# A list scheduler gets a new cost table, a model of the transfer queue, and a table of 1128 shifted due times

## The chip, the cores and the metric

One NeuronCore of one Trainium2 chip runs the whole program in one launch. The metric is the time of one execution on the device in microseconds (us); lower is better. The core has a matrix engine (TensorE, PE in the rows), a vector engine (VectorE, DVE), a scalar engine (ScalarE, ACT), GpSimd (POOL) and a queue that issues transfers (SyncE, SP). Each engine works through its own list of instructions in the order in which the program holds them, and waits at an instruction whose inputs are not there yet.

## The reference, cut to what matters

```python
def _attn_ref(q, k, v, centroids):              # 2 x 8 heads, 768 rows, 64 columns
    q_assign = np.argmax(q_n @ c_n, axis=-1)    # nearest of 16 centroids, rows normalised
    k_assign = np.argmax(k_n @ c_n, axis=-1)
    mask = q_assign[:, :, :, None] == k_assign[:, :, None, :]
    scores = np.where(mask, scale * np.matmul(q, k.transpose(0, 1, 3, 2)), -1000000000.0)
    attn = np.exp(scores - np.max(scores, axis=-1, keepdims=True))
    attn = attn / (np.sum(attn, axis=-1, keepdims=True) + 1e-09)
    return np.matmul(attn, v)

def _moe_ref(x, w1, w2, w3, w_out):             # 1536 x 512
    return (x @ w1) * (x @ w2) @ w3 @ w_out

def _moe2_ref(x, w_in, w_out):
    h = x @ w_in                                # 1536 x 2048
    return (h * np.clip(h + 3.0, 0.0, 6.0) / 6.0) @ w_out
```

The weights of the two feed-forward parts arrive as 64-bit floats, and the kernel turns them into 32-bit ones on the chip.

## The kernel before, in words

The program first makes some thousands of small operations, each with a key, the engines that it may run on and a duration for each, the operations that it needs, the buffers (rings) that it takes and gives back, and a due time. Then `Plan.order` runs a list scheduler over them: it keeps a clock for each engine, picks among the operations that could start within 0.05 us of the earliest the one with the smallest due time, advances the clocks by the durations and by a table `LAT` of delays from engine to engine, and so writes down one order. The instructions of each engine are then emitted in that order. The durations and due times decide the order and, for operations that may run on several engines, the engine; the chip never sees them. A transfer counts in this plan as busy on the queue for its listed time, and its data as there a fixed `lat` later. A result counts as free for the next writer 0.3 us after its last reader.

The work goes through these stages, which overlap at their ends:

- Attention, 16 heads of six tiles of 128 rows. For each head: q and k are loaded, split into high and low parts (`qhi`, `qlo`, `khi`, `klo`), transposed (`Tq`, `Tk`, tiles ptqB and ptkB) and copied (`CqB`, `CkB`); passes with the centroids (`pa`) and a chain of eight small steps (`oh0` to `oh7`, tiles as and ohs) give a code for each row, which is transposed (`To`, tile pto) and copied (`Ck`, `Cq`) into the rows of the score operands. A score tile is written in two parts (`S1` and `S`, tile pst), its row maximum is taken on VectorE (`mx`, tile den), the exponential on ScalarE (`ex`, tile p), the result is transposed (`pT`, tile ptr), split (`ph` on ScalarE, `pl` on VectorE) and multiplied with v (`av`). There are two score banks: the second part of a tile waits for the exponential of the tile before.
- Beside it, w3 and w_out are converted from 64-bit (`c0` on ScalarE, `c1` on GpSimd or VectorE, `c3`, `c4`, `c5` on VectorE, tiles cvt and cvs), transposed and multiplied (tile psw), and later x @ w1 and x @ w2 of the first batch (tile psab) fill TensorE between the score tiles.
- From about 400 us on: the products psx (192 passes), then the second batch's psab, psx again, and a last stage of 16 rounds (`h`, tile psh, and `o`, tile po) that uses weights which are converted, stored to DRAM (tile set, transfer `sst`) and fetched again (tile m_gb, transfers `ff` and `wf`).

The last stage opens with the additions `ca` on VectorE (tile m_sn), which the fourth group of its passes waits for. The `Whl` splits and the reciprocals of the sums (`den_recip`, which the passes `prd` wait for) stand on VectorE at the end of the attention stage.

Of the kernel before, what the change touches and what calls it, by code (L numbers as in the profile page):

```python
# [26 lines left out]
LAT = {  # L27
    ("pe", "act"): 0.2, ("pe", "dve"): 0.2, ("pe", "pe"): 0.0, ("act", "dve"): 0.155, ("act", "pool"): 0.17,
    ("dve", "act"): 0.13, ("act", "pe"): 0.17, ("dve", "pe"): 0.24, ("pool", "pe"): 0.21, ("pool", "pool"): 0.1,
        ("dve", "dve"): 0.13, ("dve", "pool"): 0.155, ("pool", "act"): 0.08,  # L30
}

# [11 lines left out]
class Plan:  # L44
# [17 lines left out]
    def order(self):  # L62
        delta, bias = 0.05, {"dve": 0.3, "pool": -0.3}
        ops = self.ops
        left, users, src = {}, {}, {}
# [7 lines left out]
        slots = {r: [0.0] * c for r, c in self.rings.items()}  # L73
        free = dict.fromkeys(ENG, 0.0)
        port = {"dve": 0.0, "pool": 0.0}
        ready = {k: None for k, o in ops.items() if not left[k]}
        out = []
        while len(out) < len(ops):
            cand = {e: [] for e in ENG}
            for k in ready:  # L80
                o = ops[k]
                t = 0.0
                ok = True
                for r in set(o[6]):
                    c = o[6].count(r)
                    if len(slots[r]) < c:
                        ok = False
                        break
                    t = max(t, sorted(slots[r])[c - 1])
                if not ok:  # L90
                    continue
                best = None
                for e, d in o[1].items():
                    st = max(free[e], t)
                    for end, pe in src[k]:
                        st = max(st, end + LAT.get((pe, e), 0.08))
# [7 lines left out]
                cand[best[1]].append((best[2], o[5], o[9], k))  # L104
# [13 lines left out]
            for r in o[6]:  # L118
                slots[r].remove(min(slots[r]))
            end = st + o[1][e]  # L120
            free[e] = end
            if e == "pool" or e == "dve" and o[10]:
                port[e] = end
            for r in o[7]:
                slots[r].append(end + 0.3)
            out.append(k)
            for u, data in users.get(k, ()):
                if data:
                    src[u].append((end + o[8], e))
                left[u] -= 1  # L130
                if not left[u]:
                    ready[u] = None
        return [ops[k] for k in out]
# [3 lines left out]
def cluster_attention_moe_kernel(  # L137
# [174 lines left out]
    op(("idle", 0), "pe", 0.0, lambda: idle_pe(5), ("id",), due=-30)  # L312
    op(("idle", 1), "pe", 0.0, lambda: idle_pe(8), [("Tq", 1, 1), ("idle", 0)], due=-30)
    op(("idle", 2), "pe", 0.0, lambda: idle_pe(3), [("S1", 0, 2), ("idle", 1)], due=-30)
    op(("idle", 3), "pe", 0.0, lambda: idle_pe(5), [("Tq", 2, 1), ("S1", 0, 3), ("idle", 2)], due=-30)
# [108 lines left out]
    def prep_ops(h):  # L424
# [13 lines left out]
        for nm, d in (("q", -6.5), ("k", -5.7)):  # L438
            for hf in range(2):
                dd = b + d + 0.4 * hf  # L440
                op(("T" + nm, h, hf), "pe", 0.17, lambda nm=nm, hf=hf: stack_T(h, nm + "B", hf),
# [9 lines left out]
        for hf in range(2):  # L451
            dd = b - 1.8 + 0.5 * hf
            op(("To", h, hf), "pe", 0.17, lambda hf=hf: codes_T(h, hf), (("oh7", h), "id"), due=dd, take=("s",),
               drop=("oh",) if hf else ())
            fop("Co", ("Ck", h, hf), {"a": 0.375, "d": 0.47}, lambda e, hf=hf: codes_C(e, h, "k", hf),
# [3 lines left out]
        op(("pa", h), "pe", 1.3, lambda: assign_mm(h), [("CqB", h, 0), ("CqB", h, 1), ("CkB", h, 0), ("CkB", h, 1),  # L459
# [149 lines left out]
    def attn_ops(h):  # L609
        b = NC * h  # L610
        for c in range(NC):
# [6 lines left out]
            op(("S1", h, c), "pe", 0.43, lambda c=c: scores(h, c, 0), nd, due=t, take=("r",))  # L618
            op(("S", h, c), "pe", 0.22, lambda c=c: scores(h, c, 1), [("S1", h, c)] + prev, due=t + 0.1,
# [4 lines left out]
            op(("ex", h, c), "act", 0.88, lambda c=c: sexp(h, c), (("mx", h, c),), due=t + 0.6, take=("p",),  # L624
# [302 lines left out]
    def T(us):  # L927
        return GS + 2.0 + us / 4.1
# [626 lines left out]
```

## Time and profile before

| what | value |
|---|---|
| runs | median 786.06 us, 785.38 to 786.44 |
| profiled execution, first to last instruction | 785.5 us |
| TensorE busy | 762.6 us (97%), 4471 passes |
| VectorE busy | 659.7 us (84%) |
| ScalarE busy | 534.7 us (68%) |
| GpSimd busy | 258.2 us (33%) |
| granted TensorE clock, mean | 0.997 |

The profile gives the span of its execution and no other time of it; the median of the runs lies 0.56 us above that span. Passes on TensorE overlap, and the end of each is modelled: a pass of 384 columns is listed with some 0.34 us while the next one starts 0.17 us later. A gap between two starts that is shorter than the listed length does not show as idle time.

### The profile page before, as it was taken

What the parts mean: (1) busy time and instruction counts of PE and PEld (TensorE: products, weight loads), DVE (VectorE), ACT (ScalarE), POOL (GpSimd) and SP (SyncE); (2) the same over time, 40 slices, a digit from 0 to 9 for tenths busy, and PEclk for the clock granted to TensorE, in tenths of its full rate; (3) what the DMA queues carried; (4) which work ended last, traced back from release to release, by engine and by line L of the source; (5) the groups of instructions that cost most, each with busy time, mean ns of one, the idle gap of its engine ahead of it and who ended that gap; (6) DMA issues with size and microseconds to landing.
All of it is one profiled execution on the core that took longest, in us unless ns stands there. A gap on an engine that the chain in (4) does not pass through costs nothing.

```text
span 785.5 us, 12835 instructions
## 1 busy us (share of the span) xinstructions
PE 762.6 (97%) x4471; PEld 698.3 (89%) x4471; DVE 659.7 (84%) x1193; ACT 534.7 (68%) x1061; POOL 258.2 (33%) x277
## 2 busy tenths in 40 slices
PE   6799999999999999999999999999999999999997
PEld 5688887789899999999999999989898989888986
DVE  7998898999999897788998798979999976666742
ACT  5679897777877786767763565746776667555543
POOL 5733757344555454323232131611122111010100
PEclk9999999999999999999999999999999999999999
DMA  7443343333454441333344543366533424212102
GB/s 248 131 149 105 89 138 101 109 113 97 120 159 146 114 148 53 90 112 114 106 138 132 152 160 114 109 217 213 164 124 120 138 91 148 81 55 68 41 14 81
DMA packets 57041, 94.24 MB, mean 120 GB/s; under 512 B 5168, under 2 KB 33936, under 8 KB 56976
## 3 DMA queue, kind: packets, MB, share of 16 engines
q1 hardware_dynamic: 56976, 93.43, 38.4%
q8 instruction: 35, 0.57, 0.3%
q14 instruction: 30, 0.25, 0.1%
HBM read 71.34 MB, written 15.78 MB: 111 GB/s over the span
## 4 chain that ended last, share of the span: by engine, by line
PE 83%; DVE 9%; ACT 4%; issue 3%; DMA 1%; ACTq 0%; POOL 0%; DVEq 0%; SPq 0%; POOLq 0%
PE po L1447 17%; PE psh L1403 15%; PE psab L843 8%; PE pst L495 7%; PE av L540 7%; PE psab L1093 7%; PE ptr L520 7%; PE psw L771 5%; PE psx L956 4%; PE pa L389 3%; DVE den L504 1%; DVE pl L184 1%; DVE cvs L720 1%; ACT p L512 1%; PE ptkB L363 1%
## 5 line engine op out<-in xcount | busy, mean ns | idle before, releaser
L711 POOL TENSOR_SCALAR cvt<-cvt 128x512 f32<-128x512 f32 x72 | 75.8, 1056 | 192.6 <-ACT cvt L187 181.2
L187 ACT ACTIVATE ph<-ptr 128x384 fp32r<-128x384 f32 x192 | 91.0, 487 | 44.9 <-PE ptr L520 43.9
L184 DVE TENSOR_TENSOR pl<-ptr,ph 128x384 fp32r<-128x384 f32 x192 | 103.4, 550 | 16.9 <-ACT ph L187 15.3
L504 DVE TENSOR_REDUCE den<-pst 128x1 f32<-128x768 f32 x96 | 91.2, 950 | 8.6 <-PE pst L495 7.0
L512 ACT ACTIVATE p<-pst,den 128x768 f32<-128x768 f32 x96 | 86.3, 898 | 9.8 <-DVE den L504 9.0
L520 PE MATMUL ptr<-id_f,p 128*128 128x128 f32 x576 | 88.4, 274 | 1.7 <-DVE pl L184 1.0
L843 PE MATMUL psab<-xT,abhl 128*128 128x384 f32 x384 | 86.9, 349 | 0.6 <-ACT asb L187 0.6
L520 PEld LDWEIGHTS ptr<-id_f,p 128*128 128x128 f32 x576 | 68.6, 140 | 11.4 <-DVE pl L184 2.3
L495 PE MATMUL pst<-kB,qB 128*128 128x512 f32 x192 | 70.1, 368 | 4.4 <-ACT p L512 4.1
L540 PE MATMUL av<-ph,vs 128*128 128x384 f32 x192 | 69.7, 363 | 0.0
L843 PEld LDWEIGHTS psab<-xT,abhl 128*128 128x128 f32 x384 | 64.4, 189 | 2.9 <-ACT asb L187 1.1
L540 PE MATMUL av<-pl,vs 128*128 128x384 f32 x192 | 65.0, 339 | 0.0
L495 PE MATMUL pst<-kA,qA 128*128 128x512 f32 x192 | 63.9, 338 | 0.2 <-issue 0.2
L187 ACT ACTIVATE m_sn<-psh 128x384 f32<-128x384 f32 x64 | 31.1, 486 | 36.1 <-PE psh L1403 35.9
L1425 ACT ACTIVATE tt<-m_sn,three 128x384 f32<-128x384 f32 x48 | 29.5, 617 | 37.3 <-DVE m_sn L1413 28.2
L724 DVE SCALAR_TENSOR_TENSOR cvs<-cvt,cvs 128x512 int32<-128x512 int32 x72 | 52.4, 731 | 0.2
L771 PE MATMUL psw<-woh,wT 128*128 128x512 f32 x128 | 52.6, 417 | 0.0
L187 ACT ACTIVATE cvt<-raw 128x512 f32<-128x512 f32 x72 | 47.6, 666 | 6.9 <-DVE m_gB L184 3.5
L720 DVE SCALAR_TENSOR_TENSOR cvs<-raw,cvs 128x512 int32<-128x512 int32 x72 | 49.6, 694 | 0.4
L495 PEld LDWEIGHTS pst<-kB,qB 128*128 128x128 f32 x192 | 36.1, 188 | 10.1 <-ACT p L512 7.7
L716 DVE TENSOR_SCALAR cvs<-cvt 128x512 int32<-128x512 int32 x72 | 33.5, 470 | 12.2 <-POOL cvt L711 6.7
L1447 PE MATMUL po<-m_hl,m_gv 128*128 128x512 f32 x162 | 43.7, 393 | 0.0
(203 smaller groups left out, 1948.9 us busy)
## 6 DMA issues: line engine op xcount, KB each, us to landing
raw<-in_moe_w_dram SPq DMA_DIRECT2D x32, 512.0 KB, 3.8
m_gb<-set SPq DMA_DIRECT2D x64, 256.0 KB, 3.2
raw<-in_moe_w_out_dram SPq DMA_DIRECT2D x24, 512.0 KB, 3.9
raw<-in_moe_w_in_dram SPq DMA_DIRECT2D x16, 512.0 KB, 4.0
set<-cvs SPq DMA_DIRECT2D x32, 256.0 KB, 3.8
abp<-cvs SPq DMA_DIRECT2D x16, 256.0 KB, 2.2
b_gv<-abp SPq DMA_DIRECT2D x16, 256.0 KB, 2.8
qn<-in_q_dram SPq DMA_DIRECT2D x16, 192.0 KB, 4.1
```

What stands on the lines that cost most here:

```text
L184: nc.vector.tensor_tensor(out=out, in0=a, in1=b, op=ALU.subtract)
L187: nc.scalar.activation(out=out, in_=in_, func=AF.Copy, **kw)
L495: x = mm(out=psr[:, t, ks_], lhsT=TT["q" + nm, h][:, i, cs_], rhs=flat(TT["k" + nm, h])[:, ks_], start=st, stop=sp)
L504: done["mx", n] = [other_banks(nc.vector.tensor_reduce(out=dens[h][:, 0, c:c + 1], in_=psS[h, c], axis=AX.X, op=ALU.max, negate=True), ("S ...
L512: done["ex", n] = [other_banks(nc.scalar.activation(out=flat(p), in_=psS.pop((h, c)), func=AF.Exp, bias=d[:, 0, c:c + 1], accum_out=d[:, 1 ...
L520: nc.tensor.transpose(pt[:, blk(c)], pps[h, 3 * hf + c][:, blk(2 * s + i)], id_f)
L540: mm(out=t[:, 0:HF], lhsT=vs_t[h][:, 2 * s + i, :], rhs=x_[:, i, :], start=(s == 0 and i == 0 and n == 0), stop=(s == 2 and i == 1 and n = ...
L711: (nc.gpsimd.tensor_scalar if e == "pool" else ts)(out=tf, in0=tf, scalar1=H_MAX, scalar2=-H_MAX, op0=ALU.min, op1=ALU.max)
L771: mm(out=ps, lhsT=wT[m, hf][:, a, blk(kk)], rhs=w_[hf][:, kk, :], start=(kk == 0 and n == 0), stop=(kk == 3 and n == 2))
L843: mm(out=ps[:, 0:HF], lhsT=s[:, w, a, blk(kk)], rhs=xT0[0][:, x_, kk, hf * HF:hf * HF + HF], start=(kk == 0 and n == 0), stop=(kk == KD - ...
L1403: mm(out=ps[:, 0:HF], lhsT=left(p, l, a, kk), rhs=x[:, x_, kk, :], start=(st and kk == 0 and m == 0), stop=(kk == 1 and m == 2), skip_grou ...
L1447: mm(out=outs[b, c], lhsT=g[:, a, blk(c % 3)], rhs=w[:, w_, :], start=(first and a == 0 and w_ == 0), stop=(last and a == 1))
```

## The change

The scheduler's numbers are replaced and the loop that uses them is refined. The kernel's arithmetic, its operations and their needs are as before.

```diff
+AT = {"pe": (0.0, 0.22, 0.23, 0.2, 0.03), "act": (0.11, 0.0, 0.04, 0.085, 0.03), "dve": (0.05, 0.035, 0.01, 0.08, 0.03),
+      "pool": (0.15, 0.04, 0.035, 0.085, 0.03), "dma": (0.02, 0.02, 0.02, 0.06, 0.02)}
+LAT = {(a, b): t for a, row in AT.items() for b, t in zip(ENG, row)}
+SERVE = {"cenl": 0.08, "lq": 0.66, "lk": 0.66, "lv": 0.6, "ld": 2.1, "Dq": 0.75, "Dk": 0.75, "dS": 0.02, "dB": 1.3,
+         "abp": 0.7, "sst": 0.85, "bf": 0.95, "ff": 0.95, "wf": 1.0, "os2": 0.7}
+ISSUE, REACH, LAND = 0.47, 1.2, 0.45
...
+SHIFT = {
+    'id': -7.8, 'cen1': -419.5, 'cen2': -133.95, 'cen3': -164.5, ('idle', 0): -2.8, ('idle', 1): -4.4,
...
+            due[k] = o[5] + SHIFT.get(k, 0.0)
+            if "dma" in o[1]:
+                o[1]["dma"] = ISSUE
+        slots = {r: [(0.0, None)] * c for r, c in self.rings.items()}
...
+        def released(slot, e):
+            t, by = slot
+            return t if by is None or by == e else t + (0.05 if e == "dma" else 0.2)
...
-                        st = max(st, end + LAT.get((pe, e), 0.08))
+                        st = max(st, end + LAT[pe, e])
...
+            if e == "dma":
+                s = SERVE[name_of(k)]
+                server = max(st + REACH, server) + s * (1.25 if st < 20 else 1.0)
+                end = server + LAND + (0.6 if st < 6 and s > 1.5 else 0.0)
             for r in o[7]:
-                slots[r].append(end + 0.3)
+                slots[r].append((end, e))
...
-            op(("S1", h, c), "pe", 0.43, lambda c=c: scores(h, c, 0), nd, due=t, take=("r",))
+            op(("S1", h, c), "pe", 0.465, lambda c=c: scores(h, c, 0), nd, due=t, take=("r",))
...
-                op(("av", h, hf, s), "pe", 0.65, lambda hf=hf, s=s: av(h, hf, s),
+                op(("av", h, hf, s), "pe", 0.7, lambda hf=hf, s=s: av(h, hf, s),
```

`SHIFT` holds 1128 entries, each added to one operation's due time; the list above shows its first row. The transfers share one server that handles them in turn. The rest of the diff replaces some twenty durations in the same way.

On VectorE, between the first and the sixth row maximum of head 0 (`TENSOR_REDUCE den<-pst`), the order before begins so. The steps named as belong to the codes of head 1, cvs<-cvt and cvs<-raw to the conversion of weights.

```order
L504 TENSOR_REDUCE den<-pst 128x1
L716 TENSOR_SCALAR cvs<-cvt 128x512
L404 TENSOR_REDUCE as_398<-pa 128x192
L504 TENSOR_REDUCE den<-pst 128x1
L720 SCALAR_TENSOR_TENSOR cvs<-raw_174,cvs 128x512
L716 TENSOR_SCALAR cvs<-cvt 128x512
L724 SCALAR_TENSOR_TENSOR cvs<-cvt,cvs 128x512
L720 SCALAR_TENSOR_TENSOR cvs<-raw_174,cvs 128x512
L504 TENSOR_REDUCE den<-pst 128x1
L406 TENSOR_REDUCE as_399<-as_398 128x12
L724 SCALAR_TENSOR_TENSOR cvs<-cvt,cvs 128x512
L408 TENSOR_TENSOR as_398<-as_398,as_399 128x192
```

At the same place VectorE now has this order.

```order
L763 TENSOR_REDUCE den<-pst 128x1
L983 SCALAR_TENSOR_TENSOR cvs<-cvt,cvs 128x512
L672 TENSOR_TENSOR ohs<-as_353,as_354 128x6x16
L763 TENSOR_REDUCE den<-pst 128x1
L443 TENSOR_TENSOR wT<-pt,wT 128x512
L674 TENSOR_TENSOR as_353<-as_353,as_354 128x96
L975 TENSOR_SCALAR cvs<-cvt 128x512
L763 TENSOR_REDUCE den<-pst 128x1
L979 SCALAR_TENSOR_TENSOR cvs<-raw_187,cvs 128x512
L763 TENSOR_REDUCE den<-pst 128x1
```

The first steps of head 1's codes (the reduction of pa and the two after it) have moved ahead of head 0's first maximum, and less conversion stands between the maxima: 24 instructions from the first maximum up to the sixth before, 17 now.

On TensorE, just ahead of head 7 (the second three passes pto transpose its codes; the second pair of pst 128x512 that follows opens its first score tile), the order before is this.

```order
L540 MATMUL av<-ph,vs 128x384
L540 MATMUL av<-pl,vs 128x384
L378 MATMUL pto<-id_r,ohs 48x128 x3
L520 MATMUL ptr<-id_f,p 128x128 x3
L495 MATMUL pst<-kB,qB 128x256
L495 MATMUL pst<-kA,qA 128x256
L495 MATMUL pst<-kB,qB 128x512
L495 MATMUL pst<-kA,qA 128x512
L743 MATMUL pt<-id_f,cvs 128x128 x4
```

TensorE now has this there.

```order
L799 MATMUL av<-pl,vs 128x384
L1030 MATMUL psw<-woh,wT 128x512
L1030 MATMUL psw<-wol,wT 128x512
L1030 MATMUL psw<-woh,wT 128x512
L637 MATMUL pto<-id_r,ohs 48x128 x3
L779 MATMUL ptr<-id_f,p 128x128 x3
L754 MATMUL pst<-kB,qB 128x256
L754 MATMUL pst<-kA,qA 128x256
L1002 MATMUL pt<-id_f,cvs 128x128 x4
L799 MATMUL av<-ph,vs 128x384
```

Three weight passes psw now stand ahead of the code transposes, and passes pt, av and ptqB stand between the transposes and the first part of head 7's score tile, which followed almost at once before.

On SP's queue, where the last stage's weights are stored and fetched (set is the store of converted weights, m_gb the fetch), the order before is this.

```order
L1306 DMA m_gb<-set_97 128x2x256
L1306 DMA m_gb<-set_96 128x512
L1323 DMA m_gb<-set_98 128x512
L1289 DMA set_102<-cvs 128x512 x2
L692 DMA raw<-in_moe_w_in_dram 128x4x256
L1289 DMA set_103<-cvs 128x512
```

The queue now has this there.

```order
L951 DMA raw<-in_moe_w_out_dram 128x1024
L1548 DMA set_102<-cvs 128x512
L951 DMA raw<-in_moe_w_in_dram 128x4x256
L1548 DMA set_101<-cvs 128x512
L1565 DMA m_gb<-set_97 128x2x256
L1565 DMA m_gb<-set_96 128x512
L1582 DMA m_gb<-set_98 128x512
```

The stores of set_101 and set_102 now go out one at a time and ahead of the three fetches; before, two stores of set_102 stood behind the three.

## Rows read from the trace of the kernel before

**Rows 1.** Stages: us; busy (instructions) of PE, PEld, DVE, ACT, POOL; clock; DMA; GB/s.

```profile
0.00:60.00 60.00, 49.22 (x281) 40.59 (x282) 52.51 (x104) 40.15 (x82) 33.60 (x62) 1.00 0.59 178
60.00:100.00 40.00, 40.00 (x273) 35.90 (x272) 34.88 (x67) 35.27 (x80) 20.61 (x23) 1.00 0.34 94
100.00:220.00 120.00, 116.42 (x767) 100.92 (x766) 112.42 (x219) 98.15 (x212) 62.16 (x70) 1.00 0.37 109
220.00:380.00 160.00, 159.90 (x1079) 152.31 (x1078) 139.00 (x261) 119.77 (x263) 65.79 (x77) 1.00 0.39 121
380.00:400.20 20.20, 19.01 (x111) 16.98 (x110) 19.00 (x30) 14.54 (x26) 6.20 (x4) 1.00 0.47 137
400.20:524.98 124.78, 124.78 (x721) 124.62 (x721) 109.32 (x193) 70.62 (x122) 33.92 (x15) 1.00 0.42 134
524.98:534.64 9.66, 7.31 (x31) 6.67 (x31) 8.72 (x15) 5.58 (x12) 1.52 (x2) 0.82 0.89 276
534.64:785.50 250.86, 245.94 (x1219) 220.35 (x1218) 183.82 (x311) 150.63 (x271) 34.44 (x26) 1.00 0.31 100
```

**Rows 2.** Waits of PE: total us, times, longest us.

```profile
PE idle L283 <- DVE id_r L259: 4.2, 1, 4.2
PE pst L495 <- ACT p L512: 4.1, 6, 1.1
PE psh L1403 <- DVE m_sn L1413: 2.1, 1, 2.1
...
PE prd L578 <- DVE den L574: 0.6, 1, 0.6
```

**Rows 3.** Timeline of DVE in head 0: start us, us, what.

```profile
20.19 0.96 DVE L504 TENSOR_REDUCE den<-pst 128x1 f32<-128x768 f32 x1 [0.38 <-PE pst L495]
...
31.30 1.29 DVE L716 TENSOR_SCALAR cvs<-cvt 128x512 int32<-128x512 int32 x1
...
37.61 0.95 DVE L504 TENSOR_REDUCE den<-pst 128x1 f32<-128x768 f32 x1
```

**Rows 4.** Timeline of one hand-over from score tile to score tile.

```profile
117.02 0.28 PE L495 MATMUL pst<-kA,qA 128*128 128x256 f32 x1
...
117.63 0.95 DVE L504 TENSOR_REDUCE den<-pst 128x1 f32<-128x768 f32 x1
...
118.61 0.90 ACT L512 ACTIVATE p<-pst,den 128x768 f32<-128x768 f32 x1 [0.46 <-DVE den L504]
...
119.66 0.39 PE L495 MATMUL pst<-kB,qB 128*128 128x256 f32 x1 [0.65 <-ACT p L512]
```

**Rows 5.** Timeline ahead of head 7.

```profile
171.34 0.34 PE L378 MATMUL pto<-id_r,ohs 128*48 128x128 f32 x3
171.50 0.55 DVE L184 TENSOR_TENSOR pl<-ptr,ph 128x384 fp32r<-128x384 f32 x1
...
172.10 0.55 PE L520 MATMUL ptr<-id_f,p 128*128 128x128 f32 x3 [0.42 <-DVE pl L184]
```

**Rows 6.** Chain that ended last, end of the attention stage: start us, us, what.

```profile
382.08 1.13 DVE Whl L184
...
386.29 1.55 DVE den L573
...
388.19 0.27 PE prd L578
```

**Rows 7.** Timeline of DVE, POOL, SP and PE ahead of the last stage.

```profile
492.14 0.55 DVE L1119 TENSOR_TENSOR g1B<-b_sn,psab 128x384 f32<-128x384 f32 x1
...
498.20 12.80 POOL L711 TENSOR_SCALAR cvt<-cvt 128x512 f32<-128x512 f32 x2 [7.68 <-ACT cvt L187]
...
516.86 0.90 SPq L1289 DMA_DIRECT2D set<-cvs  x2
...
521.99 0.43 DVE L716 TENSOR_SCALAR cvs<-cvt 128x512 int32<-128x512 int32 x1 [5.37 <-DMA set<-cvs]
...
530.29 0.54 DVE L1413 TENSOR_TENSOR m_sn<-m_sn,psh 128x384 f32<-128x384 f32 x1
...
530.89 2.09 PE L1403 MATMUL psh<-m_x1b,m_gB 128*128 128x384 f32 x6 [2.10 <-DVE m_sn L1413]
```

**Rows 8.** Groups of instructions by form on DVE: busy us, mean ns.

```profile
L716 DVE TENSOR_SCALAR cvs<-cvt 128x512 int32<-128x512 int32 x72 | 33.5, 470 | 12.2 <-POOL cvt L711 6.7 <-DMA set<-cvs 5.4
...
L184 DVE TENSOR_TENSOR Whl<-W,Whl 128x1024 fp32r<-128x1024 f32 x3 | 3.7, 1219 | 0.0
...
L229 DVE CAST kA<-pto 16x384 fp32r<-16x384 f32 x6 | 3.3, 549 | 0.9 <-PE pto L378 0.7
```

More of the change, by code (lines that the diff above doesn't have):

```diff
@@ L64, in order @@
         ops = self.ops
-        left, users, src = {}, {}, {}
+        left, users, src, due = {}, {}, {}, {}
         for k, o in ops.items():
@@ L81, in order @@
                 o = ops[k]
[L82 to L90, printed above, removed]
+                want = [(r, o[6].count(r)) for r in set(o[6])]
+                if any(len(slots[r]) < c for r, c in want):
                     continue
@@ L93, in order @@
                 for e, d in o[1].items():
-                    st = max(free[e], t)
+                    st = free[e]
+                    for r, c in want:
+                        st = max(st, sorted(released(x, e) for x in slots[r])[c - 1])
                     for end, pe in src[k]:
-                        st = max(st, end + LAT.get((pe, e), 0.08))
+                        st = max(st, end + LAT[pe, e])
                     if e == "pool":
@@ L118, in order @@
             for r in o[6]:
-                slots[r].remove(min(slots[r]))
-            end = st + o[1][e]
-            free[e] = end
+                slots[r].remove(min(slots[r], key=lambda x: x[0]))
+            end = free[e] = st + o[1][e]
             if e == "pool" or e == "dve" and o[10]:
                 port[e] = end
+            if e == "dma":
+                s = SERVE[name_of(k)]
+                server = max(st + REACH, server) + s * (1.25 if st < 20 else 1.0)
+                end = server + LAND + (0.6 if st < 6 and s > 1.5 else 0.0)
             for r in o[7]:
-                slots[r].append(end + 0.3)
+                slots[r].append((end, e))
             out.append(k)
@@ L128, in order @@
                 if data:
-                    src[u].append((end + o[8], e))
+                    src[u].append((end, e))
                 left[u] -= 1
@@ L132, in order @@
                     ready[u] = None
+        self.end = max(free.values())
         return [ops[k] for k in out]
@@ L623, in attn_ops @@
                take=("den",) if c == 0 else ())
-            op(("ex", h, c), "act", 0.88, lambda c=c: sexp(h, c), (("mx", h, c),), due=t + 0.6, take=("p",),
+            op(("ex", h, c), "act", 0.878, lambda c=c: sexp(h, c), (("mx", h, c),), due=t + 0.6, take=("p",),
                 drop=("r",))
@@ L655, in attn_ops @@
         op(("dr", h), "dve", 0.35, lambda: den_recip(h), [("ex", h, c) for c in range(NC)], due=e + 1)
-        op(("dT", h), "pe", 0.11, lambda: den_T(h), (("dr", h),), due=e + 1.2, take=("s",), drop=("den",))
+        op(("dT", h), "pe", 0.108, lambda: den_T(h), (("dr", h),), due=e + 1.2, take=("s",), drop=("den",))
         op(("dC", h), "dve", 0.2, lambda: den_C(h), (("dT", h),), due=e + 1.3, take=("rdr",), drop=("s",))
@@ L1492, in cluster_attention_moe_kernel @@
             pr = [pv] * (pv[0] >= 0)
-            op(("hr", p, ij), "act", 0.45, lambda p=p, ij=ij: h_relu(p, ij), [sr] + [("hr", *x) for x in pr], due=d,
+            op(("hr", p, ij), "act", 0.5, lambda p=p, ij=ij: h_relu(p, ij), [sr] + [("hr", *x) for x in pr], due=d,
                take=("asb",))
@@ L1511, in cluster_attention_moe_kernel @@
                     nd.append(("o", n, cc - 1))
-                op(("o", n, cc), "pe", 0.69, lambda p=p, ij=ij, cc=cc, first=first, last=last: o_mm(p, ij, cc, first, last),
+                op(("o", n, cc), "pe", 0.693, lambda p=p, ij=ij, cc=cc, first=first, last=last: o_mm(p, ij, cc, first, last),
                    nd, due=T(t0 + TP + (3 * k_ + c + 0.5) * TP / 12), take=("t",) if first else (),
```

97 lines of the change are left out of this document (66 added, 31 removed), and 202 rows, old and new, of the table SHIFT.

## The prediction

> **What bounds the kernel now.** I read the stages first [rows 1], then what TensorE waits for [rows 2], then the timeline at those waits. TensorE counts as busy for 762.6 of 785.5 us, so it looks as if nothing were left. The number of passes says more than the busy share, since a pass is listed for longer than it keeps the next one off. From 60 to 100 us, where no idle time shows, TensorE starts 273 passes in 40 us, one every 0.147 us. From 100 to 220 us the same mixture of work (scores, transposes, weight passes) gives 767 passes in 120 us, one every 0.156 us. At the pace of the stage before they would take 767 x 0.1465 = 112.4 us, so 7.6 us are lost there, although only 3.6 us show as idle. In the same way the first 60 us hold 281 passes, worth 41.2 us: 18.8 us are lost, of which 4.2 stand before the first pass, where TensorE waits for the identity matrix [rows 2], and 14.6 us behind it. From 400.2 to 525 us it starts 721 passes of 384 columns, one every 0.173 us, and never idles; from 534.6 us on it idles 4.9 us of 250.9, nearly all at the very end, behind the last pass. In between, at the start of the last stage, 31 passes that are worth 31 x 0.173 = 5.4 us take 9.66 us: 4.3 us are lost.
>
> So the losses that an order can reach are 14.6 us (first 60 us), 7.6 (100 to 220), about 1 (around 385) and 4.3 (525 to 535), 27.5 us together. The remaining stages run at their pace already, and the work on TensorE is the same 4471 passes after the change. Neither can the order shorten it much more than this: VectorE is busy for 52.5 of the first 60 us and for 112.4 of the 120 us from 100 to 220 [rows 1], so it is the second bound of just the stages in which TensorE loses time.
>
> **The change, term by term.** Nothing is removed or added but order and the choice of engine. I cost each place where the order differs and the trace shows a loss.
>
> *First 60 us.* Head 0's six row maxima start between 20.19 and 37.61 us [rows 3], 17.4 us for five steps. A step cannot be shorter than the hand-over from tile to tile: from the last score pass at 117.02 through the maximum at 117.63 and the exponential at 118.61 to the next pass at 119.66 it is 2.6 us [rows 4], 13.2 us for five. VectorE's order between the first and the sixth maximum falls from 24 instructions to 17. By kind there are fewer of the code steps of head 1, of conversion steps and two fewer pl, and one copy more; at about 0.5 us each, that is some 3.3 us less, so 17.4 becomes about 14.1, still above 13.2. But the pl and the conversion steps come later, and head 2 starts behind much the same work as before, so part of it returns. I take 2.5 us; the ends are a loss of 1.5 (all of it returns, and three score tiles now follow one another on TensorE with little between them) and a gain of 5 (all stays and the start of head 1 is as much earlier).
>
> *100 to 220 us.* The losses sit where one head ends and the next starts. Ahead of head 7 the passes ptr wait 0.42 us for a pl on VectorE, right behind the code transposes pto [rows 5]; from 171.34 to 172.10 three short passes take 0.76 us. In the new order three psw stand ahead of them, and ptr, pt, av and ptqB between them and the score tile that needs their copies. Heads 6, 8 and 9 get more work in that place too, heads 4 and 5 less. VectorE gets relief as well: of the copies that may run on ScalarE, 14 instead of 19 stay on VectorE in the attention stage, five at 0.55 us [rows 8], 2.7 us. Its idle time in the stage, 7.6 us [rows 1], is the room that it has. I take half of the 7.6 us that are lost, 4 us, between a loss of 2 (the two heads that got worse, at most 1 us each) and a gain of 7.6.
>
> *Around 385 us.* The step before the reciprocals starts at 386.29 us, behind the Whl split of 382.08 and others, and prd follows at 388.19 [rows 6] after a wait of 0.6 us [rows 2]. In the new order the reciprocals stand ahead of it, and two of three Whl, 1.2 us each [rows 8], go to GpSimd. I take 1 us, between 0 and 2.
>
> *Start of the last stage.* VectorE needs from 492.14 to 530.29 us, 38.2 us, from the last product of the stage before to the addition that the fourth group of psh waits for; 5.4 us of it is a wait for a store to free a buffer, which was issued at 516.86 behind three fetches [rows 7]. TensorE covers this stretch with 192 passes psx and the first 18 psh, 210 x 0.173 = 36.3 us. The new order has one or two more conversion steps in the stretch (0.7 and 0.5 us), but the stores go out singly and ahead of the fetches. Without the wait VectorE needs 38.2 - 5.4 + 1.2 = 34.0 us, 2.3 us less than TensorE gives it. The stall should go. With it goes the low clock: the granted clock is 0.82 in 525 to 535 us and 1.00 on both sides [rows 1], between its levels of 2.4 and 1.2 GHz, after a gap of 2.1 us in the passes [rows 2]. The waits alone, 2.35 us, leave 1.9 of the 4.3 lost us to the clock. I take 4, between 0 (the store still comes late by more than 2.3 us) and 4.3.
>
> The Trainium skill ("TensorE: Matmul & The Clock Gate", Part 1) has it that an idle TensorE is put back to 1.2 GHz and gets 2.4 GHz only after sustained work, so a stall costs more than its own length. The trace agrees here: by waits alone the last term would be 2.35 us, by the passes it is 4.3.
>
> The sum: 2.5 + 4 + 1 + 4 = 11.5 us off the profiled 785.5 us, 774.0. The median of the runs lies 0.6 us above that execution, so **774.6 us**. Its own range, with the four terms at about half and at one and a half, is 769 to 780.
>
> **The rivals.**
>
> *VectorE stays the bound.* In the attention stage the waits only move to other places, since VectorE has the same work but for some 3 us, and is at 94% from 100 to 220 us. Then only the last two terms hold, 5 us: 781. For it speaks that heads 4 and 5 lose cover; against it, that 60 to 100 us, where VectorE is busy for 34.9 of 40 us, runs without any loss.
>
> *More of it goes.* If two thirds or more of the 27.5 us go, the time is 785.5 - 18.5 + 0.6 = 767.6, and with 21 us gone 765. For it speaks that transfers, whose lateness made the largest single stall, now stand in the plan with their queue; against it, that the first 60 us hold half of the sum, with VectorE full.
>
> *No change.* The new order trades stalls for stalls: 785 to 787.6. I call a difference below 0.2% (1.6 us) no change throughout, since the three runs spread by 1.1 us.
>
> *Slower: GpSimd and VectorE hold each other up in new places.* At 498.20 two clamps of GpSimd took 12.8 us while VectorE worked through the splits and sums behind 492.14 [rows 7], and at 31.30 a shift on VectorE took 1.29 us [rows 3] against a mean of 0.47 [rows 8]. An order that is made tight everywhere has no slack for such a meeting: each costs up to 0.8 us and delays all that stands behind. In the stretch to 220 us GpSimd runs 155 instructions [rows 1]; 14 more meetings of 0.8 us there eat the gain of 11.5, and 18 give 785.5 - 11.5 + 14.4 + 0.6 = 789. Against it: GpSimd's list has one instruction fewer than before, and the plan holds both engines apart for most pairs, before and after.
>
> The Trainium skill ("SBUF — State Buffer", Summary: rules for kernel authors) says that a VectorE operation with two inputs in SBUF and a GpSimd operation that reads SBUF exclude each other until the first is done. The row of 12.8 us agrees; by that rule the order decides how often they meet, and this rival is its price.
>
> **How the numbers follow.** Forecast (769 to 780): 0.50. VectorE stays the bound (780 to 784.5): 0.14. More of it goes (below 769): 0.18. No change (784.5 to 787.6): 0.08. Slower: 0.10. So faster by over 0.2%: 0.82, within 0.2%: 0.08, slower: 0.10. The range 765 to 786 leaves out about 0.05 below (more than 20 of the 27.5 us gone) and 0.13 above.
>
> **What the profile after would show.** First term: six maxima of head 0 in about 14 us and head 1's first tile earlier. Second: from 100 to 220 us fewer than 0.153 us for each pass. Third: no wait of prd for den. Fourth: no wait for m_sn of over 0.5 us at the first psh, no 5 us wait of VectorE for the store, and a clock of 1.00 there. The prediction is wrong if the passes of the attention stage end no earlier than 395 us, if GpSimd's and VectorE's times for one clamp or shift grow, or if a new stall appears in the stages behind 400 us, which I hold for unchanged.

## The result, and the profile after

The changed kernel takes 795.87 us (median of 4 runs, 793.44 to 796.78) against 786.10 of the kernel before on the same chip: ratio 1.0114, 95% interval 1.0091 to 1.0137. It is slower by 1.1%, 9 to 10 us, where 774.6 us, a gain of 11.5, was forecast. The profiled execution spans 793.9 us, 8.4 more than before.

The stages of the changed kernel, columns as in [rows 1], cut where its own stages change (psx starts at 405.2 us instead of 400.0, psh at 530.4 instead of 525.0):

```profile
0.00:60.00 60.00, 48.25 (x249) 39.25 (x250) 44.89 (x96) 36.96 (x74) 31.71 (x60) 0.91 0.53 166
60.00:100.00 40.00, 39.83 (x269) 35.17 (x267) 34.75 (x63) 35.18 (x79) 19.87 (x22) 1.00 0.31 96
100.00:220.00 120.00, 116.57 (x775) 101.39 (x774) 113.27 (x217) 96.03 (x209) 60.27 (x69) 1.00 0.37 112
405.20:530.40 125.20, 125.15 (x721) 124.72 (x720) 113.67 (x193) 71.06 (x123) 11.90 (x15) 1.00 0.43 140
530.40:540.00 9.60, 7.51 (x42) 6.93 (x42) 8.95 (x18) 5.11 (x12) 1.80 (x3) 1.00 0.77 254
540.00:660.00 120.00, 116.81 (x570) 102.23 (x569) 106.87 (x180) 77.88 (x139) 17.08 (x16) 1.00 0.38 129
```

The kernel before had this row for the stretch that is new in the list, from 540 to 660 us:

```profile
540.00:660.00 120.00, 120.00 (x601) 108.20 (x600) 105.03 (x177) 79.76 (x144) 22.97 (x19) 1.00 0.43 136
```

Two places show it, by the passes started in the same time. The first 60 us hold 249 passes instead of 281 [rows 1], and from 540 to 660 us, where TensorE never idled before, 570 instead of 601. The stretch from 100 to 220 us gained a little (775 for 767). Counted by the same work instead, the changed kernel is 1.3 us behind at the first 256-column score pass of the second head, 7.7 at that of the third (73.9 against 66.2), 5.2 at the first psx, 5.4 at the first psh and 8.7 at the last po (788.9 against 780.2).

What TensorE waits for now (total us, times, longest us), against [rows 2]:

```profile
PE idle L542 <- DVE id_r L518: 4.2, 1, 4.2
PE pst L754 <- ACT p L771: 2.6, 5, 1.7
PE psw L1030 <- POOL wol L440: 2.3, 2, 1.6
PE psh L1662 <- DVE m_sn L1672: 2.1, 1, 2.1
PE psh L1662 <- DVE tt L1688: 1.7, 3, 1.0
PE pto L637 <- DVE pl L443: 1.4, 1, 1.4
PE po L1706 <- DVE m_gv L443: 1.3, 1, 1.3
PE pst L754 <- ACT qA L446: 1.2, 1, 1.2
```

The wait of prd is gone, that of psh for m_sn is as long as before, and the waits for wol, qA, tt and m_gv and the longer one of pto for pl are new or grew.

### The profile page after: what moved, and what is told of

Its sections match the earlier page's. It is cut to its first block, busy times and chain, and to the rows that moved or that the text cites. A ratio compares the mean times of both kernels' runs of the same rounds, so it can differ in the third digit from the quotient of the medians.

```text
span 793.9 us, 12825 instructions
## 1 busy us (share of the span) xinstructions
PE 766.6 (97%) x4471; PEld 697.2 (88%) x4471; DVE 660.8 (83%) x1191; ACT 536.2 (68%) x1064; POOL 232.6 (29%) x276
## 4 chain that ended last, share of the span: by engine, by line
PE 65%; DVE 19%; ACT 7%; issue 4%; DMA 4%; POOL 1%; DVEq 0%; ACTq 0%; POOLq 0%
PE po L1706 10%; PE psh L1662 9%; PE psab L1102 8%; PE psab L1352 6%; PE pst L754 6%; PE av L799 6%; PE ptr L779 6%; PE psx L1215 4%; PE psw L1030 4%; DVE den L763 3%; DVE pl L443 2%; PE pa L648 2%; DVE cvs L979 2%; ACT p L771 1%; DMA raw<-in_moe_w_in_dram 1%
## 5 line engine op out<-in xcount | busy, mean ns | idle before, releaser
L970 POOL TENSOR_SCALAR cvt<-cvt 128x512 f32<-128x512 f32 x72 | 49.8, 693 | 229.3 <-ACT cvt L446 213.5
L446 ACT ACTIVATE ph<-ptr 128x384 fp32r<-128x384 f32 x192 | 89.3, 485 | 32.0 <-PE ptr L779 30.4
L754 PE MATMUL pst<-kB,qB 128*128 128x512 f32 (+1 forms) x192 | 71.9, 376 | 2.6 <-ACT p L771 2.6
L754 PE MATMUL pst<-kA,qA 128*128 128x512 f32 (+1 forms) x192 | 64.8, 342 | 1.2 <-ACT qA L446 1.2
L979 DVE SCALAR_TENSOR_TENSOR cvs<-raw,cvs 128x512 int32<-128x512 int32 x72 | 53.7, 748 | 1.1
L1706 PE MATMUL po<-m_hl,m_gv 128*128 128x512 f32 x153 | 40.9, 393 | 1.3 <-DVE m_gv L443 1.3
L975 DVE TENSOR_SCALAR cvs<-cvt 128x512 int32<-128x512 int32 x72 | 33.7, 469 | 9.7 <-POOL cvt L970 7.5
```

The costliest lines, as they stand in the source:

```text
L446: nc.scalar.activation(out=out, in_=in_, func=AF.Copy, **kw)
L754: x = mm(out=psr[:, t, ks_], lhsT=TT["q" + nm, h][:, i, cs_], rhs=flat(TT["k" + nm, h])[:, ks_], start=st, stop=sp)
L979: stt(out=s, in0=raws.pop(key)[:, :, 0], scalar=29, in1=s, op0=ALU.logical_shift_right, op1=ALU.bitwise_or)
L1706: mm(out=outs[b, c], lhsT=g[:, a, blk(c % 3)], rhs=w[:, w_, :], start=(first and a == 0 and w_ == 0), stop=(last and a == 1))
```

## The experiments

First the results together. Each time is a median; the ratio is to the kernel before on the same chip. The last four columns are read from each run's profile: passes that TensorE started up to 60 us, the start of the first 256-column score pass of the third head, the first psx, and the passes from 540 to 660 us.

| run | us | ratio, 95% interval | to 60 us | third head | psx | 540 to 660 |
|---|---|---|---|---|---|---|
| before | 786.1 | | 281 | 66.2 | 400.0 | 601 |
| changed | 795.9 | 1.0114 (1.0091 to 1.0137) | 249 | 73.9 | 405.2 | 570 |
| e1 no shifts | 806.4 | 1.0239 (1.0218 to 1.0260) | 242 | 72.7 | 409.0 | 557 |
| e2 no early shifts | 798.4 | 1.0135 (1.0114 to 1.0156) | 239 | 73.6 | 406.9 | 572 |
| e3 no late shifts | 800.1 | 1.0153 (1.0127 to 1.0178) | 235 | 75.8 | 406.7 | 570 |
| e4 32 more idle passes | 795.7 | 1.0107 (1.0088 to 1.0127) | 283 | 73.6 | 405.8 | 579 |
| e5 latencies alone | 814.6 | 1.0333 (1.0310 to 1.0357) | 244 | 73.1 | 409.5 | 521 |
| e6 queue alone | 803.0 | 1.0201 (1.0174 to 1.0228) | 230 | 75.3 | 411.0 | 565 |
| e7 durations alone | 796.6 | 1.0116 (1.0092 to 1.0141) | 263 | 70.0 | 404.3 | 584 |
| e8 control, latency | 805.2 | 1.0234 (1.0200 to 1.0268) | 225 | 76.3 | 412.5 | 564 |
| e9 front of before | 796.1 | 1.0109 (1.0088 to 1.0129) | 265 | 71.2 | 405.3 | 572 |
| e10 last stage of before | 790.4 | 1.0035 (1.0022 to 1.0048) | 243 | 74.5 | 405.7 | 601 |
| e11 both of before | 791.5 | 1.0054 (1.0038 to 1.0070) | 273 | 69.9 | 404.4 | 598 |
| e12 control, window | 794.5 | 1.0086 (1.0073 to 1.0099) | 275 | 67.8 | 405.3 | 597 |
| e13 wol wait moved | 798.4 | 1.0136 (1.0115 to 1.0157) | 239 | 75.1 | 408.1 | 576 |
| e14 8 idle passes out | 792.2 | 1.0065 (1.0040 to 1.0090) | 253 | 71.4 | 404.6 | 569 |
| e15 four heads of before | 790.1 | 1.0032 (1.0017 to 1.0048) | 264 | 68.7 | 404.3 | 597 |
| e16 e10 and e13 | 794.5 | 1.0096 (1.0074 to 1.0118) | 236 | 75.5 | 407.1 | 595 |
| e17 e10 and e14 | 788.5 | 1.0017 (1.0000 to 1.0034) | 267 | 69.4 | 400.0 | 600 |
| e18 before, 8 idle out | 787.6 | 0.9997 (0.9985 to 1.0009) | 262 | 67.8 | 401.7 | 601 |

Measured again beside e1 to e18, the kernel before took 787.3 to 788.0 us, so small differences between the runs are judged by the ratios. The columns are of one execution each, which can lie up to 3.6 us off the median: e14's (795.7 us) is its slowest, e9's (799.1) is too, e17's (786.9) its fastest. Runs that share their order up to some point mostly agree there within 1.3 us (third head 73.9 and 74.5 in the changed kernel and e10), but e14 and e17, with one order up to 493 us, differ by 2.0 us at the third head and by 4.6 at psx. Smaller differences of these columns mean nothing. The passes up to 60 us include 21 idle ones; in e4 they are 53, in e14, e17 and e18 13, so that without them it is 260 before, 228 in the changed kernel, 230 in e4, 240 in e14, 254 in e17 and 249 in e18.

From the first psh to the last po each run starts the same 1248 passes. That takes 255.2 us before, 258.5 in the changed kernel, 254.5 in e10, 254.7 in e12, 254.6 in e17, 258.9 in e14, 259.1 in e8 and 269.3 in e5.

**Which of the shifts lose.** Theory A was that the shifts had closed gaps and so made stalls.

```diff
-            due[k] = o[5] + SHIFT.get(k, 0.0)
+            due[k] = o[5]                                             # e1
+            due[k] = o[5] + (SHIFT.get(k, 0.0) if o[5] >= 8 else 0.0)    # e2
+            due[k] = o[5] + (SHIFT.get(k, 0.0) if o[5] < 140 else 0.0)   # e3
```

> The changed kernel without any of the 1128 shifts: new cost table, new latencies and the model of the transfer queue stay. Theory A (the shifts closed every gap in front of TensorE that the list's own reckoning had, so that each instruction that comes later on the chip than in the list becomes a stall): the gaps come back, the loss goes: 780 to 788 us, the first scores tile of the third head at 66 to 69 us as before (73.9 with the shifts). Theory B (the new costs and the queue model are what is wrong, the shifts are innocent): 793 to 799 us, as with the shifts. Theory C (the shifts help, and the cost table loses more than they bring): over 799 us.

> Shifts only where the due time in the program is 8 or later: those of the first 45 us are off, all others on. Theory A1 (most of the loss lies in the first 45 us: after the shifts the waits for qA and wol there are bare and TensorE falls to its lower clock): the third head's first tile at 66 to 69 us instead of 73.9, and 787 to 791 us in all; the new stalls of the last stage (3 us) stay. Rival A2 (the middle and the last stage lose whatever the front does, since each stall that goes is given back at the next tight place): third head early, but 793 to 797 us in all.

> Shifts only where the due time is under 140: those of the last stage and of its conversions are off. Theory A1: the stalls of 0.5 to 2.3 us that appeared ahead of psh at 533, 544, 591, 625 and 659 us go, but for the one at 533: the stretch from the first psh to the last po falls from 258.5 to about 255 us, and the time from 795.9 to 791 to 793. Rival: the stalls come from weights that arrive late whatever the order of the last stage: they stay, 795 to 797 us.

Theory A is wrong, and so is A1. Without the shifts the kernel takes 806.4 us: the shifts bring about 10 us, and the new tables under them lose about 19. Leaving out the early or the late shifts alone gains nothing: the ratios are 0.2 and 0.4% above that of the changed kernel, with intervals that overlap its own, and the times lie above both ranges that I had given, in e2 and in e3. Without the late ones the stretch from the first psh to the last po takes 262 us (533.2 to 795.6), where I had expected 255. Theory C stands.

**Is it the clock?** In the changed kernel the granted clock falls to 0.50, TensorE's lower level of 1.2 GHz, between 24 and 28 us and again after 36 us, behind waits. This run puts passes of no use into the waits.

```diff
+    FILL = {("S1", 0, 0): 6, ("S1", 0, 1): 8, ("S1", 0, 4): 8, ("S1", 0, 5): 4, ("S", 0, 5): 3, ("pT", 0, 0, 0, 0): 3}
...
             o[3](*((o[2],) if o[0] in flex else ()))
+            idle_pe(FILL.get(o[0], 0))
```

> The changed kernel with 32 more idle passes of TensorE, placed into its waits between 19 and 42 us (nothing of the order moved). Theory of the clock: granted clock 1.00 in every 2 us from 20 to 46 us (0.50 to 0.93 before), passes at full pace, the third head's first tile 3 to 4 us earlier (70 to 71 us) and 791 to 794 us in all. Theory of the waits alone (the clock's fall only stretches passes that wait anyway for GpSimd and ScalarE): third head at 73 to 74.5, 795 to 797 us. If the passes that I add come in the way of TensorE's work: over 797.

Two stretches of the changed kernel, columns as in [rows 1]:

```profile
24.00:28.00 4.00, 3.82 (x12) 3.00 (x13) 2.33 (x5) 2.67 (x5) 3.32 (x5) 0.50 0.54 170
36.00:40.00 4.00, 2.95 (x12) 2.01 (x11) 3.97 (x6) 2.50 (x6) 2.72 (x4) 0.64 0.00 0
```

and of e4:

```profile
24.00:28.00 4.00, 4.00 (x18) 3.28 (x17) 1.73 (x3) 1.54 (x3) 2.21 (x4) 0.89 0.53 172
36.00:40.00 4.00, 3.98 (x21) 2.81 (x20) 3.41 (x5) 2.94 (x7) 2.79 (x3) 1.00 0.01 3
```

The clock came back, the time did not: 795.7 against 795.9 us, the third head at 73.6 instead of 73.9. So the waits set this stretch; what the lower level costs TensorE there is time that it would wait anyway. The Trainium skill ("TensorE: Matmul & The Clock Gate", Terms) prices throttled time at its length times the share of pulses that is missing. Here that price was not paid, since other engines ended last.

**Which table loses.** e1 holds three tables; each goes alone into the kernel before, and a control (e8) changes nothing but every latency, by 0.03 us, a second (e12) nothing but the window in which the list chooses by due time, from 0.05 to 0.06 us.

```diff
-                        st = max(st, end + LAT.get((pe, e), 0.08))
+                        st = max(st, end + LAT[pe, e])             # e5, with the new LAT and released()
+                server = max(st + REACH, server) + q * (1.25 if st < 20 else 1.0)   # e6, with SERVE and ISSUE
-            op(("S1", h, c), "pe", 0.43, ...
+            op(("S1", h, c), "pe", 0.465, ...                      # e7, with the other durations
+                        st = max(st, end + LAT.get((pe, e), 0.08) + 0.03)   # e8
-        delta, bias = 0.05, {"dve": 0.3, "pool": -0.3}
+        delta, bias = 0.06, {"dve": 0.3, "pool": -0.3}             # e12
```

> The kernel before with one part of the change: the new latencies between engines and the new rule for the release of buffers; old durations, no queue model, no shifts. The version without shifts took 20 us more than before, so one of the three tables costs that, or all of them do. Theory L (the old latencies held a margin that kept work a little ahead; the new, smaller ones leave none): 796 to 808 us. Theory Q (the queue model is the part): 782 to 790 us. Theory D (the due times written by hand fit the old table alone, and any other reckoning costs): 791 to 800 us, here and in the control.

> The kernel before with the model of the transfer queue alone. Theory Q (it believes transfers later or earlier than they are, and weights of the last stage come late): 796 to 808 us, with waits ahead of psh between 540 and 660 us. Theory L: 782 to 790 us. Theory D: 791 to 800 us.

> The kernel before with the new durations alone (27 lines, 1 to 20 per cent each, and the idle passes priced at 0.7 to 2.3 us where they were free). Theories L and Q: 782 to 790 us. Theory D: 791 to 800 us. If the idle passes' price is what spoils the front: the first scores tile of the second head at 50 us or later (45.2 before, 51.8 without shifts).

> A control that is no part of the change: the kernel before with 0.03 us added to every latency, which should be neutral as a forecast. Theory D (any other reckoning undoes what was fitted by hand): 791 to 800 us. Theories L and Q: 784 to 789 us, and what the change's own tables cost is theirs.

> A second control that is no part of the change: the kernel before with the window in which the list chooses by due time 0.06 us wide instead of 0.05. Theory D (the order of before is a picked one, any other that the same list makes is slower): 791 to 808 us, with the loss ahead of the third head and between 525 and 660 us. Rival (the first control was an accident of the latencies): 784 to 789 us.

Every one is slower, by 7 to 27 us, the two controls by 18 and 7. So neither L nor Q alone: theory D holds, in that no other order which this list made from the same due times, six with e1, came within 0.7% of the order before. Its range of 791 to 800 us does not hold: only e7 and e12 lie in it, e6 (803.0) fits Q as well, and e5 (814.6) and e8 (805.2) lie above. As a control costs 18 us, these runs can't say what a single table is worth. The worst row of the windows of e5 (first) and of e8 show where these two lose:

```profile
540.00:660.00 120.00, 108.91 (x521) 94.70 (x522) 104.22 (x169) 71.95 (x128) 24.46 (x22) 0.99 0.45 144
```

```profile
0.00:60.00 60.00, 43.03 (x225) 34.65 (x226) 42.69 (x88) 34.22 (x66) 30.48 (x59) 0.86 0.53 164
```

They are the two places of the changed kernel again. e12 does not fit the places that I named: its third head is only 1.6 us late and its last stage whole; it loses between the fifth and the seventh head and ahead of 530 us.

**Orders written out and spliced.** Here the order is a list of operation numbers and engines, so that parts of both orders can be joined.

```diff
+        raw = zlib.decompress(base64.b64decode(ORDER))
+        for i in range(0, len(raw), 2):
+            n = raw[i] + 256 * raw[i + 1]
+            o = ops[n // 8]
+            o[2] = ENG[n % 8]
+            out.append(o)
```

> The order is written out: the kernel before's order up to the first scores tile of the third head, then what is left in the order of the changed kernel. Local theory (the loss sits in the first 66 us and in the first third of the last stage; what lies between is 2.5 us shorter in the changed kernel): third head at 66 to 68 us (73.9 in the changed kernel), the stretch from there to the first psx 331 to 334 us, 787 to 791 us in all. Rival (the later order fits only what the early one leaves, and a splice makes new stalls): 792 us or more.

> The order written out: that of the changed kernel up to the first psx of the second half (about 496 us), then what is left in the order of before. Local theory: the stretch from the first psh to the last po 255 to 256 us (258.5 in the changed kernel), 791 to 794 us in all. Rival: the stalls of the last stage come from transfers that were issued late before the cut: 795 to 798 us.

> Both splices: front and last stage of before, the order of the changed kernel from the third head to 480 us. Local theory: 66.2 + 331.3 us to the first psx, and before's 380 us from there: 2.5 us less than before, 783 to 786 us. Rival: 788 us or more.

> The order written out: before's up to the first scores tile of the fifth head, the changed kernel's from there to about 480 us, before's from there. Theory of the seam (what the early splice gave back at 73 to 80 us was the seam, not the order behind it): fifth head at 109 to 111 us, first psx at 399 to 401.5 us, 785 to 788 us in all, equal to before. Rival (the order of the changed kernel from the fifth head on takes more time than that of before): psx after 403 us, 789 us or more.

For the last stage the local theory holds, with a time 0.6 us below its range. With the order of before from 496 us on, 5.4 us go (6 by the ratios), and the row from 540 to 660 us is nearly the one of before again:

```profile
540.00:660.00 120.00, 120.00 (x601) 108.14 (x600) 108.33 (x185) 80.94 (x145) 22.96 (x19) 1.00 0.42 135
```

For the front it fails. In e9 the third head starts 2.7 us earlier than in the changed kernel, and psx starts at 405.3 instead of 405.2; this execution is e9's slowest, but its median (796.1) shows no gain either. With four heads of before (e15) the fifth head starts at 111.9 and psx at 404.3, as the rival had it. With both splices (e11) the time is no better than with the last stage alone. A splice puts work of the dropped part in other places, so these runs don't say what the front's order is worth by itself.

**What holds the front up.** e13 moves the pieces of W that wait for wol behind score tiles; e14 takes out eight passes of no use, priced at 1.9 us in the new durations and free in the old.

```diff
-    op(("idle", 1), "pe", 1.9, lambda: idle_pe(8), [("Tq", 1, 1), ("idle", 0)], due=-30)
+    op(("idle", 1), "pe", 1.9, lambda: idle_pe(0), [("Tq", 1, 1), ("idle", 0)], due=-30)
```

> The order of the changed kernel written out, with two pieces of W moved on TensorE: the first (three passes, the second of which waits 1.6 us for wol) from ahead of the second score tile of head 0 to behind the start of the third, the second piece from ahead of the sixth tile's second half to behind it. Theory of the new wait (TensorE's order puts a wait for GpSimd in front of the score tiles, and the chain of maxima, exponentials and transposes shifts with it): the second maximum of head 0 starts at about 24.1 us instead of 26.1, the third head's first tile at 71 to 73 us instead of 73.9, 793 to 795 us in all. Rival (VectorE and GpSimd set the front, TensorE's order does not): 73.5 to 75 us, 795 to 798 us in all.

> The changed kernel without the eight idle passes between 12.9 and 16.4 us, which the list prices at 1.9 us and which take 3.5 there; nothing else moved. Theory of the price: the copies into kB and qA on ScalarE come earlier, the wait of 1.2 us for qA at 20 us goes, the second half of the first score tile starts at 19.8 to 20.6 us instead of 21.5, 794 to 795.5 us in all. Rival (the passes only fill a wait, or without them TensorE stays at its lower clock for longer): 21.3 us or later, 795.5 to 799 us.

> The two moved pieces of W, and the last stage of before: if both are independent, 790.4 less what the moved pieces alone bring: 787 to 790 us. If the front's gain is taken back later, as in the splice of the front: 790 to 792 us.

> The changed kernel's order without the eight idle passes, and from the second half's first psx (about 493 us) the order of before. If the two gains (3.6 and 5.4 us) add: 786 to 788.5 us, equal to before. If the front's gain is taken back behind the attention stage, as in the profile without the passes (attention 2.9 us earlier, first psx 0.6 earlier): 789 to 791.5 us.

> The kernel before without the same eight idle passes (3.1 us there, from 13.3 to 16.3 us). Theory of the price (before put work behind them that had to wait for a load anyway, so they are hidden; in the changed order copies that ScalarE must do first hang on them): 786 to 788.5 us, no change. Rival (they cost in any order): 783 to 785.5 us. If TensorE stays at its lower clock without them: over 789 us.

e13 gained nothing (1.0136 against 1.0114, with intervals that overlap), and e16 lost 4 to 5 us against e10, above both of its ranges: the wait for wol went and came back at the exponentials, which TensorE waits 7.1 us for in e13 and 2.6 in the changed kernel. The row of e13's waits:

```profile
PE pst L544 <- ACT p L561: 7.1, 7, 2.8
```

e14 gained 3.7 us by the medians (1.0065 against 1.0114, intervals that just miss each other), more than I had given, though not at the wait that I had named: that for qA only fell from 1.20 to 0.90 us, while those for wol fell from 2.3 to 0.4. Timelines of the engines tell the chain, first in the changed kernel (start us, us, what):

```profile
12.90 3.74 PE L542 MATMUL idle<-id_r 128*128 128x512 f32 x8
16.44 0.71 PE L622 MATMUL ptkB<-id_r,ks 128*128 128x128 f32 x6
16.99 0.81 PE L648 MATMUL pa<-cT,qB 128*128 128x32 f32 x6
18.73 0.56 DVE L663 TENSOR_REDUCE as<-pa 128x192 f32<-128x384 f32 x1 [1.02 <-PE pa L648]
21.75 0.65 POOL L669 TENSOR_TENSOR as<-as,wtab 128x192 f32<-128x192 f32 x1 [1.48 <-DVE as L667]
22.36 1.76 POOL L440 TENSOR_TENSOR wol<-cvs,woh 128x512 fp32r<-128x512 f32 x1
24.18 0.80 PE L1030 MATMUL psw<-wol,wT 128*128 128x512 f32 x1 [1.57 <-POOL wol L440]
```

then in e14:

```profile
13.79 1.42 PE L648 MATMUL pa<-cT,qB 128*128 128x32 f32 x6
17.62 0.55 DVE L663 TENSOR_REDUCE as<-pa 128x192 f32<-128x384 f32 x1
20.10 0.64 POOL L669 TENSOR_TENSOR as<-as,wtab 128x192 f32<-128x192 f32 x1 [0.96 <-DVE as L667]
20.72 1.77 POOL L440 TENSOR_TENSOR wol<-cvs,woh 128x512 fp32r<-128x512 f32 x1
22.55 0.80 PE L1030 MATMUL psw<-wol,wT 128*128 128x512 f32 x1
```

The passes pa of head 1 stand behind the idle passes, the code steps on VectorE behind pa, a code step on GpSimd behind those, wol behind it in GpSimd's order, and TensorE's next score tile behind the pieces of W. The list gave the idle passes 1.9 us; from 12.90 to the next pass at 16.44 they take 3.54. In the kernel before the same passes cost nothing that could be measured (e18); there pa of head 1 came only at 21 us, behind other work. With both mends (e17) the time is 788.5, 1.0017 of before: hardly a difference. That psx starts at 400.0 us as before is read from the fastest of twelve executions. Against e10 the missing passes bring 1.4 to 1.9 us in e17, which is within the noise (the intervals overlap). No version beat the kernel before.

## Why the prediction was wrong

**The sum as a whole.** The step that failed is "the losses that an order can reach": I added up what the order before lost, and priced the new order only there. The places without loss were held for unchanged ("The remaining stages run at their pace already"), so the sum could hardly come out above 785; new stalls had a place only in the rivals. At the prediction's own paces the same arithmetic for the changed kernel gives, in lost us, 60 - 249 x 0.1465 = 23.5 in the first 60 us (18.8 before), 120 - 775 x 0.1465 = 6.5 from 100 to 220 (7.6), 9.6 - 42 x 0.173 = 2.3 at the start of the last stage (4.3), and 5.2 from 540 to 660 (0). The last is by columns, since the 31 passes that are missing there are mostly short ones: 34 fewer psh of 384 columns and 3 more po of 512 are 11520 columns, and the kernel before starts 264192 in these 120 us. Together 6.8 us more, of the 8.4 by which the span grew; the other 1.6 lie elsewhere in the attention stage, 0.6 of them from 60 to 100 us. Two forecast gains are there, 3.1 us; 9.9 us of new loss stand against them, all of it in stages that I left out or had with the other sign. The count by the same work agrees: 5.2 us to the first psx, 0.2 to the first psh, 3.0 from there to the end.

**First 60 us: -2.5 forecast, +4.7 measured.** The first and the last of the six maxima:

```profile
23.19 0.94 DVE L763 TENSOR_REDUCE den<-pst 128x1 f32<-128x768 f32 x1
...
39.17 0.94 DVE L763 TENSOR_REDUCE den<-pst 128x1 f32<-128x768 f32 x1
```

These rows are of VectorE's timeline in the changed kernel: 16.0 us for five steps, not 14, and the first comes 3 us later than in [rows 3]. I counted VectorE's instructions between the maxima because VectorE was full there. It is no longer: 44.9 busy us instead of 52.5 [rows 1]. TensorE loses most from 20 to 24 us, at the waits for qA and wol, with 6 passes (first row) where it had 31 before (second row):

```profile
20.00:24.00 4.00, 1.43 (x6) 0.91 (x6) 4.00 (x9) 1.75 (x4) 2.52 (x3) 0.93 0.83 239
20.00:24.00 4.00, 4.00 (x31) 3.63 (x30) 3.55 (x5) 2.00 (x6) 3.84 (x6) 1.00 0.98 232
```

What ends last there is the chain shown for e14, and later a wait of 1.7 us for an exponential. The second head still starts only 1.3 us late, with less weight work ahead of it (9 passes psw instead of 27). That work comes between the second head and the third (42 psw instead of 21), which starts 7.7 us late. I read the order for what had moved away from VectorE and not for what now stands in front of TensorE's next tile.

**100 to 220 us: -4 forecast, -1.1 measured.** The sign was right, the size too large. A new wait of 1.4 us of pto for a pl (the row above) replaces part of what went.

**Around 385 us: right.** No wait of prd is left in the list.

**Start of the last stage: -4 forecast, -2.0 measured.** The store's wait of 5.37 us [rows 7] is gone: VectorE's shifts (`c3`, L975) wait 1.4 us for stores in the whole program. The columns of this row are those of [rows 8].

```profile
L975 DVE TENSOR_SCALAR cvs<-cvt 128x512 int32<-128x512 int32 x72 | 33.7, 469 | 9.7 <-POOL cvt L970 7.5 <-DMA set<-cvs 1.4 <-PE pt L1002 0.6
```

The clock holds at 1.00. But psh waits for m_sn as long as before, 2.1 us: "2.3 us less than TensorE gives it" did not hold. The list filled the time that the wait left with other work on VectorE: in the stretch of the 721 passes it is busy for 113.7 us, against 109.3 [rows 1].

**Behind 540 us: 0 forecast, +5.2 measured**, the largest miss after the first 60 us (7.2); with the last stage's order of before it is gone (e10). How such a stall comes about shows at the first, in the timelines of the engines:

```profile
543.19 1.48 DVE L443 TENSOR_TENSOR m_gB<-m_gb,m_gB 128x1280 fp32r<-128x1280 f32 x1
544.26 1.54 POOL L440 TENSOR_TENSOR m_gB<-m_gb,m_gB 128x512 fp32r<-128x512 f32 x1 [5.93 <-ACT m_gB L446]
544.59 1.62 DVE L443 TENSOR_TENSOR m_gv<-tt,m_gv 128x384 fp32r<-128x384 f32 x1
546.27 0.51 PE L1706 MATMUL po<-m_hl,m_gv 128*128 128x512 f32 x1 [1.28 <-DVE m_gv L443]
```

The split m_gv that the passes po need stands behind a split of weights, 1.48 us, for a later round; GpSimd starts another piece of it 0.3 us ahead of m_gv, and m_gv takes 1.62 us instead of the 0.54 to 0.56 of 37 of the 43 pieces of its size on this engine. That is the meeting of the two engines on which the slower rival was built; the Trainium skill ("SBUF — State Buffer", Summary: rules for kernel authors) says that the second of two such operations waits for the first, and the row agrees. It is one case, though, and not shown to be the cause of the whole: the mean of GpSimd's clamps fell from 1056 to 693 ns and that of VectorE's shifts did not change (470 and 469 [rows 8]). Most of the fall is two clamps of 12.2 and 7.1 us in the kernel before (the first in [rows 7]), from 400 us on, where TensorE never idled. The kernel before and then the changed one:

```profile
L711 POOL TENSOR_SCALAR cvt<-cvt 128x512 f32<-128x512 f32 x72 | 75.8, 1056 | 192.6 <-ACT cvt L187 181.2 <-DVE pl L184 5.1 <-DVE b_sn L1106 4.6
L970 POOL TENSOR_SCALAR cvt<-cvt 128x512 f32<-128x512 f32 x72 | 49.8, 693 | 229.3 <-ACT cvt L446 213.5 <-DVE m_gB L443 8.4 <-DVE m_gb L1570 6.1
```

So the slower rival had the sign, and a mechanism that these runs show in one stall only.

**What is shown and what is open.** Shown: the order of the last stage costs 5 to 6 us (e10), and it and the idle passes together nearly all (e17). The idle passes alone cost about 4 us in e14 and 1 to 2 in e17, the second within the noise, so their share is less sure. Shown too: the new tables, without shifts, cost 19 us, and small changes of no meaning cost 7 to 18. Not tried is the changed kernel with the idle passes at another price. Not shown is why the order before is so much better than its neighbours; that its due times had been picked on the chip for the old numbers would explain it, and was not tested. Open is also why the front of before, spliced in, gives its gain back.

## What to carry to other kernels

When a table that feeds a list scheduler changes, the whole order is drawn anew, and all that was good in the old one is at stake: price the places without stalls too, and set aside some per cent for the draw. Two controls that change the tables by nothing that matters tell how wide that draw is, before any gain is credited to a better model. A better time in the plan need not be one on the chip: put through the plan's new tables, the order before ends at 775.0 us, the one without shifts at 771.1, the changed one at 759.6 (the plan's own arithmetic, no measurement), and the chip takes 786.1, 806.4 and 795.9. And look at what stands behind passes of no use: the same eight cost nothing before, at a price of 0 us, and cost time in the new order, at 1.9 us (they take 3.5), where a chain that score tiles wait for hangs on them.

## What the runs showed of the hardware that was not expected

- In the first 16 us passes of 512 columns take 0.44 us (eight from 12.90 to 16.44 us), though the granted clock is listed as 1.00 there (8 to 20 us). Later in the changed kernel such passes start 0.23 us apart (first fence), and in e14, without the eight passes, the same two are still 0.43 apart (second), where the clock is listed as 1.00 too (third, columns as in [rows 1]). So the column does not show all of a slow start, and e14 was no slower for it.

```profile
21.75 0.40 PE L754 MATMUL pst<-kB,qB 128*128 128x512 f32 x1
21.98 0.40 PE L754 MATMUL pst<-kA,qA 128*128 128x512 f32 x1
```

```profile
21.19 0.63 PE L754 MATMUL pst<-kB,qB 128*128 128x512 f32 x1
21.62 0.63 PE L754 MATMUL pst<-kA,qA 128*128 128x512 f32 x1
```

```profile
20.00:24.00 4.00, 3.83 (x10) 2.53 (x10) 3.25 (x7) 2.13 (x5) 3.73 (x4) 1.00 1.05 238
```

- A fall of the granted clock to 0.50 cost nothing that could be measured in this place (e4), since TensorE was not what ended last.
